# Three of seven transposes moved from TensorE to VectorE, a fourth replaced by small products, and the work of the start and the loop put in a new order

## The chip, the cores and the metric

The kernel runs on one core of one Trainium2 chip. Times are device microseconds (us). The engines are called as in the profile: PE is TensorE (the matmuls), DVE is VectorE, ACT is ScalarE, POOL is GpSimd, and SP is the engine whose queue issues nearly all DMAs here. In the traces here each engine works through its own instructions in the order in which they were written and stops at the first one that has to wait; below, four pieces of work on POOL stand 37 us behind one that waits.

A kernel's time is the median of its runs. A run counts as slow when it is over 1.5% above the fastest of its kernel. The granted clock of PE is the share of its full clock that it was given, as the profile shows it. Each profile is of one execution, whose span is 1.7 to 2.2 us shorter than the time of that run; positions in time are in a profile, counted from the start of its span. There is one profile of each kernel.

## The reference

```python
def _attn_ref(r, k, v, w, a, b):            # each (4, 8, 768, 40), float32
    state = np.zeros((B, H, D, D), dtype=np.float32)
    for t in range(S):
        kt, vt, rt = (k[:, :, t], v[:, :, t], r[:, :, t])
        wt, at, bt = (w[:, :, t], a[:, :, t], b[:, :, t])
        y[:, :, t] = np.einsum('bhd,bhde->bhe', rt, state)
        Sa = np.einsum('bhde,bhe->bhd', state, at)
        state_decay = state * wt[:, :, None, :] - np.einsum('bhd,bhe->bhde', Sa, bt)
        state = state_decay + np.einsum('bhd,bhe->bhde', vt, kt)

def _moe_ref(x, w_in, w_out):               # x (3072, 320), w_in (320, 2048), w_out (2048, 320)
    h = x @ w_in
    g = 0.5 * h * (1.0 + erf(h * inv_sqrt2))
    return (g @ w_out).astype(np.float32)
```

The recurrence's y, turned to 3072 tokens by 320, is the x of the two matrix products. `w_in` and `w_out` arrive as 64-bit floats, so the kernel makes float32 of them on the chip first.

## The kernel before

The 768 steps are cut into 12 chunks of 64. Within a chunk the recurrence is a set of small matrix products and one triangular inverse. Names that the text uses:

- *N*: a masked product of chunk c. It goes out to memory, comes back as *Nb* in another layout, and POOL (DVE for chunk 0) forms the inverse column by column. The inverse goes out and comes back as *Tt*; *L*, *J* and *J2* put its blocks together.
- *X*, *sap*, *saT*, *M*, *QY*: the chain of products of a chunk, which needs the state of the one before. X(2) is the first work of the main loop, and its start marks the end of "the start" in this document.
- *ph* and *po*: the groups of the two large products of the previous chunk, four of each per iteration, which the program puts between the small ones (`fill()`).
- *RV*, *A*, *av*, *tn*, *cum*, *ks*, *nb*: further small products, transposes and scaled operands of a chunk, called here as in the kernel; *kT*, *aT* and the like are the turned (transposed) forms of k, a and so on.
- *pieces*: `w_in` is converted in ten pieces (1 to 5 its left half, 6 to 10 its right half), `w_out` in sixteen.

A piece begins on DVE and ACT and ends either on DVE or on POOL:

```python
    def to_float(dst, words, eng):
        ...
        power = work.tile([P, LW // 2], UINT32, tag="power", name="power", bufs=2)[:, :n]
        mant = work.tile([P, LW // 2], UINT32, tag="mant", name="mant", bufs=2)[:, :n]
        nc.vector.tensor_scalar(power, hi, 0x7FF00000, None, ALU.bitwise_and)
        nc.scalar.activation(power, power, ACT.Relu, bias=rebias, scale=8.0)
        nc.vector.tensor_scalar(mant, hi, 0x000FFFFF, 0x00100000, ALU.bitwise_and, ALU.bitwise_or)
        yield
        nc.vector.scalar_tensor_tensor(power, hi, 0x80000000, power, ALU.bitwise_and, ALU.bitwise_or)
        ...
        if eng is nc.vector:
            eng.scalar_tensor_tensor(mant_f, lo, 2.0 ** -32, mant, ALU.mult, ALU.add)
            eng.scalar_tensor_tensor(dst, mant_f, 2.0 ** -20, power_f, ALU.mult, ALU.mult)
        else:
            nc.scalar.mul(lo_f, lo, 2.0 ** -52)
            nc.scalar.mul(mant_f, mant, 2.0 ** -20)
            eng.tensor_tensor(mant_f, mant_f, lo_f, ALU.add)
            eng.tensor_tensor(dst, mant_f, power_f, ALU.mult)
```

`convert(n)` runs the first half of the next piece and the second half of the piece begun before; `convert(n, True)` also ends what is begun. All turned operands come from PE, eight transposes of 128x128 each, and a copy or product out of PSUM:

```python
    def flip(src, name):
        pt = duo(name).rearrange("p g (n t) -> p g n t", n=NP)
        for g in range(G):
            for n in range(NP):
                nc.tensor.transpose(pt[:, g, n], src(g, n), ident)
        return pt
```

The start around chunk 2, and the loop's edges:

```python
    convert(1)                     # a piece of w_in; others precede
    fill()                         # ph group 1 of chunk 0
    make_M(1)
    make_y2(1)
    convert(1, True)               # ends the last piece of w_in
    turns_a(2)
    fill()                         # ph group 2
    make_N(2)
    run(start_inverse(2, nc.gpsimd))
    ...
    for c in range(2, NCH):
        ...
        if more:
            make_N(n)              # n = c + 1
            run(start_inverse(n, nc.gpsimd))
        make_X(c)
        ...
        if more2:
            turns_b(n + 1)         # kT, vT, rT
        if more:
            turn_state()
        fill()                     # the last po group
        if more:
            joined(n)              # J2
```

## Time and profile before

| | before |
|---|---|
| time, median of 3 runs before the prediction | 832.77 us |
| profiled span, mean granted PE clock | 825.5 us, 0.934 |
| X(2) starts (end of the start) | 209.5 us |
| from there to the end (the loop) | 616.0 us |
| PE busy from 200 to 820 us | 597 of 620 us |

The table is read in two parts, as the two stages have different limits. In the loop PE is the bound, so the loop shortens by what PE no longer has to do or to wait for. In the start PE is idle for more than a third of the time (busy for 131 of 209.5 us), and what counts is the chain of waits across engines and queues that ends at X(2). The prediction below shows the lines.

### The profile page before, as it was taken

What the parts mean: (1) busy time and instruction counts of PE and PEld (TensorE: products, weight loads), DVE (VectorE), ACT (ScalarE), POOL (GpSimd) and SP (SyncE); (2) the same over time, 40 slices, a digit from 0 to 9 for tenths busy, and PEclk for the clock granted to TensorE, in tenths of its full rate; (3) what the DMA queues carried; (4) which work ended last, traced back from release to release, by engine and by line L of the source; (5) the groups of instructions that cost most, each with busy time, mean ns of one, the idle gap of its engine ahead of it and who ended that gap; (6) DMA issues with size and microseconds to landing.
All of it is one profiled execution on the core that took longest, in us unless ns stands there. A gap on an engine that the chain in (4) does not pass through costs nothing.

```text
span 825.5 us, 29243 instructions
## 1 busy us (share of the span) xinstructions
PE 720.1 (87%) x13262; PEld 588.3 (71%) x13262; DVE 292.3 (35%) x452; ACT 226.8 (27%) x265; POOL 317.8 (38%) x785
## 2 busy tenths in 40 slices
PE   7427588377999999998998999999999999989997
PEld 4326467255887877877876877868878878868785
DVE  3667535856332233233233233243233333211100
ACT  4102363232232233232232232222322232102010
POOL 3380044830282281570660570660751832800000
PEclk9656779778999999999999999999999999999999
DMA  9744555733632722722712722722625322020000
GB/s 134 163 84 101 140 111 114 133 96 70 104 56 41 115 49 46 130 43 41 124 30 47 123 40 39 124 46 55 100 54 87 65 48 49 12 54 3 25 10 16
DMA packets 247820, 60.36 MB, mean 73 GB/s; under 512 B 236368, under 2 KB 240976, under 8 KB 247696
## 3 DMA queue, kind: packets, MB, share of 16 engines
q1 hardware_dynamic: 247532, 58.33, 39.4%
q8 instruction: 104, 1.70, 0.9%
q14 instruction: 20, 0.16, 0.1%
q10 hardware_dynamic: 164, 0.16, 0.1%
HBM read 44.30 MB, written 10.22 MB: 66 GB/s over the span
## 4 chain that ended last, share of the span: by engine, by line
PE 56%; POOL 12%; SPq 10%; DMA 10%; DVE 5%; issue 5%; ACT 2%; POOLq 0%; DVEq 0%; ACTq 0%
PE ph L671 20%; PE po L679 16%; POOL W L492 5%; POOL tmp L490 4%; PE QY L96 3%; SPq L639 2%; SPq L142 2%; DMA inv<-W 2%; PE J L96 2%; DMA Nb<-N 2%; DMA gt<-in_moe_w_in_dram 1%; DMA N<-N 1%; POOL st L492 1%; PE N_ps L96 1%; POOL st L490 1%
## 5 line engine op out<-in xcount | busy, mean ns | idle before, releaser
L679 PE MATMUL po<-w_out_sb,gt 128*128 128x320 f32 x768 | 223.0, 445 | 6.8 <-DVE w_out_sb L245 5.6
L671 PE MATMUL ph<-xt,w_in_sb 64*128 64x256 f32 x1920 | 223.4, 386 | 0.8 <-issue 0.8
L490 POOL TENSOR_TENSOR tmp<-W,Nb 128x126 f32<-128x126 f32 (+22 forms) x310 | 113.3, 365 | 266.7 <-DMA Nb<-N 243.1
L671 PEld LDWEIGHTS ph<-xt,w_in_sb 64*128 64x128 f32 x1920 | 185.5, 190 | 24.6 <-issue 2.4
L679 PEld LDWEIGHTS po<-w_out_sb,gt 128*128 128x128 f32 x768 | 146.9, 196 | 69.2 <-DVE w_out_sb L245 8.6
L492 POOL TENSOR_TENSOR W<-W,tmp 128x126 f32<-128x126 f32 (+22 forms) x310 | 124.4, 401 | 24.3
L673 ACT ACTIVATE gt<-ph 128x1024 f32<-128x1024 f32 x48 | 49.1, 1024 | 231.4 <-PE ph L671 231.4
L683 DVE COPY os<-po 128x320 f32<-128x320 f32 x24 | 11.8, 492 | 132.2 <-PE po L679 124.7
L629 DVE TENSOR_TENSOR y<-QY,y 128x512 f32<-128x512 f32 x22 | 15.1, 687 | 77.1 <-PE QY L96 77.1
L414 DVE TENSOR_TENSOR A<-A_ps,upper 128x1024 f32<-128x1024 f32 x12 | 14.7, 1224 | 61.5 <-PE A_ps L96 61.5
L371 POOL TENSOR_TENSOR ks<-k_raw,part 128x640 f32<-128x640 f32 x11 | 21.2, 1928 | 31.7 <-ACT part L343 25.2
L414 DVE TENSOR_TENSOR SM<-M_ps,upper 128x1024 f32<-128x1024 f32 x12 | 14.7, 1224 | 52.5 <-PE M_ps L96 52.5
L96 PE MATMUL J<-L,N 32*32 32x32 f32 x768 | 9.6, 201 | 27.1 <-DVE L L529 27.1
L96 PEld LDWEIGHTS J<-L,N 32*32 32x32 f32 x768 | 8.6, 113 | 32.1 <-issue 32.1
L414 DVE TENSOR_TENSOR VR<-RV_ps,upper 128x1024 f32<-128x1024 f32 x12 | 14.7, 1224 | 47.2 <-PE RV_ps L96 47.2
L464 ACT COPY avs<-av 128x640 f32<-128x640 f32 x12 | 8.3, 692 | 80.5 <-PE av L96 80.5
L96 PE MATMUL av<-VR,A 64*64 64x40 f32 x768 | 15.3, 240 | 15.8 <-POOL st L492 14.4
L96 PEld LDWEIGHTS av<-VR,A 64*64 64x64 f32 x768 | 13.9, 149 | 20.1 <-POOL st L492 14.6
L238 ACT ACTIVATE power<-power,rebias 128x320 uint32<-128x320 uint32 (+1 forms) x26 | 16.1, 624 | 42.7 <-DVE power L237 42.7
L96 PE MATMUL RV_ps<-rT,vT 40*64 40x64 f32 x768 | 15.6, 237 | 11.1 <-ACT rT L405 11.1
L96 PEld LDWEIGHTS RV_ps<-rT,vT 40*64 40x64 f32 x768 | 13.8, 149 | 14.9 <-ACT rT L405 11.9
L382 DVE TENSOR_TENSOR aT<-aT_ps,wpT 128x1024 f32<-128x1024 f32 x12 | 14.7, 1224 | 26.8 <-ACT wpT L380 23.6
(138 smaller groups left out, 950.7 us busy)
## 6 DMA issues: line engine op xcount, KB each, us to landing
Nb<-N SPq DMA_DIRECT2D x22, 256.0 KB
v_pad<-in_v_dram SPq DMA_DIRECT2D x48, 80.0 KB
r_pad<-in_r_dram SPq DMA_DIRECT2D x48, 80.0 KB
out_dram<-os SPq DMA_DIRECT2D x48, 80.0 KB
w_raw<-in_w_dram SPq DMA_DIRECT2D x22, 160.0 KB
b_raw<-in_b_dram SPq DMA_DIRECT2D x22, 160.0 KB
a_pad<-in_a_dram SPq DMA_DIRECT2D x22, 160.0 KB
k_raw<-in_k_dram SPq DMA_DIRECT2D x22, 160.0 KB
```

Source lines behind the costliest of these rows:

```text
L96: nc.tensor.matmul(o, lhsT, rhs, start=first, stop=True, skip_group_check=True)
L142: eng.dma_start(out=t[half(e)].rearrange("p g h d -> p (g h) d")[:, g::2, :D], in_=rows[:, H * g:H * (g + 1)])
L238: nc.scalar.activation(power, power, ACT.Relu, bias=rebias, scale=8.0)
L371: nc.gpsimd.tensor_tensor(ks[:, :, :, :D], raws.pop((c, "k")), rwv, ALU.mult)
L414: nc.vector.tensor_tensor(to, pt, upper.unsqueeze(1).to_broadcast([P, 2 * G * NP, C]), ALU.mult)
L490: eng.tensor_tensor(t, W[:, :rows, j:j + 1].to_broadcast([P, rows, rest]), Nb[:, j:j + 1, j + 1:].to_broadcast([P, rows, rest]), ALU.mult)
L492: eng.tensor_tensor(W[:, :rows, j + 1:], W[:, :rows, j + 1:], t, ALU.add)
L629: nc.vector.tensor_tensor(y2, Y, y2, ALU.add)
L639: eng.dma_start(out=xt[own + n * i:own + n * (i + 1), NP], in_=xt[other + REST:other + D, i])
L671: nc.tensor.matmul(ph[:, x, s], w_in_sb[half(x), kt, p * P:(p + 1) * P], xt[half(x), kt], start=kt == 0, stop=kt == NK - 1)
L673: nc.scalar.activation(gt[:, 4 * q:4 * q + 4].rearrange("p (x s) t -> p x s t", x=2), ph, ACT.Gelu)
L679: nc.tensor.matmul(po[:, g], gt[:, f, g * P:(g + 1) * P], w_out_sb[:, f], start=f == 0, stop=f == NF - 1)
```

## The change

The intent is to take PE work out of the loop. a, v and r are loaded in another layout ("pairs") that lets DVE's 32x32 block transpose give the turned operand, straight into SBUF. The running sums of log w are no longer transposed: PE sums them in turned form, by 64 small products. The state's part of y (y2) is summed by PE into the PSUM banks of QY, so that its own copy and additions fall away. VR gets its own load of v. N of the next chunk moves to an earlier place in the loop. And the start is written anew: pieces that ended on DVE now end on POOL, and loads and stores have other places in SP's queue.

```diff
@@ the turning of operands
-        (nc.scalar.copy if c < 3 else nc.vector.tensor_copy)(vT, flip(by_place(v_), "vT_ps"))
+    def turn(to, c, n):
+        nc.vector.transpose(to.rearrange("p n (s y) -> p n y s", y=2),
+                            raws.pop((c, n)).rearrange("p n (y d) -> p n y d", y=2)[:, :, :, :BL])
...
+        pt = duo("wT_ps").rearrange("p e (n t) -> p e n t", t=C)
+        for n in range(G * NP):
+            for x in range(2):
+                for e in range(2):
+                    at = (2 * n + x) * D
+                    mm(pt[half(x), e, n], logw[half(e), at:at + HP], cum_m[half(e), half(e)])
...
@@ y2, in the banks of QY (make_QY then adds to them: first=False)
-        pt = duo("y2_ps").rearrange("p g (i e t) -> p g i e t", i=NP, e=2)
-        for g, i, x, e, q, m in units():
-            mm(pt[half(x), g, i, e], tn[half(g, D), e, i, half(x)], t["rT"][half(g, D), q, m, half(e)])
-        y2 = t["y2"] = side("y2", "late", 1)
-        nc.scalar.copy(y2, pt.rearrange("p g i e t -> p g i (e t)"))
+                        mm(t["QY"][g][half(x), e, i, D:], tn[half(g, D), e, i, half(x)],
+                           t["rT"][half(g, D), i // NA, 2 * (i % NA) + x, e], i == 0)
...
@@ the start, around chunk 2
-    first_pieces((4,), 1, nc.vector)
-    first_pieces((0, 1, 2, 3), 1, nc.gpsimd)
+    first_pieces(range(NK), 1, nc.gpsimd)
...
+    fill()
+    make_N(2)
+    run(start_inverse(2, nc.gpsimd))
     convert(1)
     fill()
-    make_M(1)
     make_y2(1)
-    convert(1, True)
-    turns_a(2)
-    fill()
-    make_N(2)
-    run(start_inverse(2, nc.gpsimd))
+    make_M(1)
+    convert(1)
...
+    turn_k(2)
+    convert(1, True)
...
@@ the loop
-        if more:
-            make_N(n)
-            run(start_inverse(n, nc.gpsimd))
         make_X(c)
...
         if more2:
-            turns_b(n + 1)
-        if more:
-            turn_state()
+            turn_k(n + 1)
+            make_N(n + 1)
+            run(start_inverse(n + 1, nc.gpsimd))
         fill()
```

## The prediction

> **What bounds the kernel now.** I first read the forty slices, for the stages.
>
> ```profile
> PE   7427588377999999998998999999999999989997
> POOL 3380044830282281570660570660751832800000
> PEclk9656779778999999999999999999999999999999
> ```
>
> A slice is 20.6 us. TensorE (PE) is over 90% busy at full clock from slice 11 on, and sparse at a reduced clock before that. So there are two stages with different limits. The sums over stretches (length, then busy us of PE, PEld, DVE, ACT, POOL, then clock, DMA share, GB/s) put sizes on them:
>
> ```profile
> 140.00:200.00 60.00, 34.62 (x352) 23.80 (x350) 43.70 (x86) 17.23 (x25) 28.89 (x65) 0.74 0.55 119
> 200.00:820.00 620.00, 597.18 (x10996) 491.30 (x10997) 173.60 (x216) 160.73 (x179) 239.64 (x606) 0.99 0.34 59
> ```
>
> From 200 us on, PE works 597 of 620 us, and no other engine reaches 40%: a loop bound by PE, where only PE work removed is time removed. Between 140 and 200 us PE works 35 of 60 while DVE works 44: that stage waits for the conversion of the second weight matrix on DVE.
>
> Second, the PE groups, for what the loop's PE time is made of (count | busy us, mean ns | idle before):
>
> ```profile
> L96 PE MATMUL saT_ps<-Tt,part 64*64 64x64 f32 x704 | 14.3, 231 | 0.0
> L351 PE MATMUL rT_ps<-ident,r_pad 128*128 128x128 f32 x96 | 13.4, 286 | 5.9 <-DMA r_pad<-in_r_dram 5.9
> L351 PE MATMUL vT_ps<-ident,v_pad 128*128 128x128 f32 x96 | 12.6, 274 | 3.2 <-DMA v_pad<-in_v_dram 3.2
> L351 PE MATMUL aT_ps<-ident,a_pad 128*128 128x128 f32 x88 | 11.5, 274 | 2.1 <-DMA a_pad<-in_a_dram 2.0
> ```
>
> These means overlap in time; what counts is the pace from one group's start to the next. At full clock the PE timeline gives vT at 439.82, rT at 440.70, tn at 441.57: 0.87 us for eight transposes. A group of 64 small matmul records (saT, N, RV, M) takes 1.09 us in the chain. One iteration sums to about 56.7 us of such paces (ph 18.1, po 17.4, seven transposes 6.2, the rest 15), and iterations follow each other after 58 to 63 us; the difference is a wait of 1.29 us at J in nearly every one, plus instruction-issue gaps of 1 to 1.6 us in some.
>
> Third, the start, from the timelines of POOL, PE and DVE:
>
> ```profile
> 125.22 1.27 POOL L250 TENSOR_TENSOR w_in_sb<-mant,power 128x512 f32<-128x512 f32 x1
> 126.42 0.53 POOL L480 MEMSET W<- 128x512 f32 x1
> ...
> 137.76 0.24 POOL L490 TENSOR_TENSOR tmp<-W,Nb 128x31 f32<-128x31 f32 x1 [10.47 <-DMA Nb<-N]
> ...
> 168.34 0.23 POOL L492 TENSOR_TENSOR W<-W,tmp 128x16 f32<-128x16 f32 x1
> ```
>
> ```profile
> 127.09 4.59 PE L671 MATMUL ph<-xt,w_in_sb 64*128 64x256 f32 x40
> ...
> 134.62 4.59 PE L671 MATMUL ph<-xt,w_in_sb 64*128 64x256 f32 x40
> ```
>
> ```profile
> 127.21 1.23 DVE L414 TENSOR_TENSOR N<-N_ps,upper 128x1024 f32<-128x1024 f32 x1 [1.37 <-PE N_ps L96]
> ```
>
> Before, POOL finishes the last piece of the first weight matrix at 126.5 us and only then begins the inverse of chunk 2; PE's third and fourth ph groups (127.09, 134.62) come right behind the pieces. The inverse starts 9.3 us after the end of the N mask (128.44 to 137.76) and takes 30.7 us while DVE is busy.
>
> **What the Trainium skill says.** "VectorE: DVE Perf Modes", The three transpose paths: VectorE transposes only 32x32 blocks, and lands in SBUF, where TensorE's transpose lands in PSUM and needs a copy. The trace has such a transpose, L: 128x512 in 0.702 us. The product-wise DVE instructions take 0.82 us for 640 columns and 1.22 for 1024, so I estimate 1.24 us for 128x1024. "SBUF — State Buffer", two separate sides: a DVE instruction with two SBUF inputs and a GpSimd instruction that reads SBUF lock each other out. The trace agrees: in the first inverse on DVE 126 columns cost 0.29 us before POOL's inverse runs beside it and 0.36 to 0.37 after. "TensorE: Matmul & The Clock Gate", why this matters: idle gaps over about 3 us bring the array back to half clock. The trace agrees: after the 8.76 us gap before RV at 152.5 us, the 1.16 us group takes 1.99.
>
> **The change, part by part.**
>
> *PE in the loop.* The transposes of a, v and r leave PE: 3 x 0.87 = 2.6 us per chunk. The turned sums are no longer 8 transposes (0.88) but 32 products of 64x64, that is 64 records like saT, 1.09: +0.2. y2 keeps its 64 records and only changes its target. Net -2.4 us for each of the 8 iterations that still prepare a later chunk: -19. One N group of 1.09 moves out of the loop into the start: -1. The last iteration's wait at J (3.36 us) should become the usual 1.3, because its N and inverse now start almost an iteration earlier: -2. Against that, two more v loads per chunk stand in the SP queue ahead of the inverse's store, about 1.5 us of issue, of which 0.8 is won back because the outputs no longer need an addition first: J waits perhaps 0.3 longer, +2 in all. Loop: -20 us.
>
> *DVE, ACT, POOL in the loop.* DVE gains a transpose and an SBUF multiply of the old length (vT and rT copies were 1.22 each already), and loses the sums' copy (0.82) and two additions (2 x 0.69). ACT loses the 1.01 us y copy, POOL two copies of 0.45. All of it lies beside PE, which is the bound: worth nothing by itself. The PSUM pair that y2 now holds earlier leaves two of four buffers for M and ph, whose readers need 1.2 us each beside products of 2.2 us or more: no wait expected.
>
> *The start.* Here the listing of the new order decides. POOL's order becomes: pieces 1 to 5 of the first weights (left half), ks of chunk 2, piece 6, then the whole inverse of chunk 2, then pieces 7 to 10. PE's third ph group needs pieces 6 to 10. So PE must wait there for N(2), its trip through memory, the inverse and four pieces. My chain, with the durations of before:
> - The first N mask ends about 16 us (17.5 before), as a and b load ahead of k; the inverse on DVE, 22.6 us, ends near 50; the first state is out near 79.5 (80.8 before).
> - DVE then does outputs 2.2, turns of v and r 2.5, L 0.7: 85. Behind it J, tn, RV, av, X, cum, turned sums, sap, saT follow on PE to about 95, then nb, the turn of a and its scaling (3.3 us), and piece 5 waits for them on DVE and ACT and ends on POOL near 105. First ph done 109 (115 before), N(2) masked 111.5 (128.4 before).
> - Inverse: + 9.3 trip + 27.5 (27.4 in chunk 1 with DVE partly busy) = 148. Four pieces of 2 x 1.28 us are 10.2, but there are two buffers of power and mant, so pieces 9 and 10 start their DVE and ACT parts only when 7 and 8 are finished: about 13. End 161.5. Rest of ph, fourth ph, QY(1): 3 + 4.5 + 3 = 172. PE has stood still about 40 us; before, it had QY(1) and the fourth ph behind it at 139.
> - From there DVE has 15 pieces of the second weights at 2.05 us (the time with POOL idle, as at 171 to 196 us; 2.75 beside an inverse) = 31, outputs 3.6, turns 2.5, masks 2.4, nb, turn and scaling of a 3.3: 43, plus some 5 of waits for raw weights (6 before). Then 9 to 10 us of J, kT, N, po, J2. X(2), the loop's first work, starts at 172 + 57 = 229 us; before it started at 209.5. Start: +19.5 us.
>
> Sum: +19.5 - 20 = about 0, on 832.8. I put it at 831.
>
> **Rivals.** *The start costs nothing*: if the new order reaches X(2) at about 210, the loop's -20 shows bare, 812 us. For it: N(2) is 16 us earlier and the conversion no longer runs beside an inverse. Against it: POOL is in order, and pieces 7 to 10 stand behind the inverse. *The DMA queue becomes the loop's bound*: a loop's loads take 16 issues before and 28 after (issues of 0.4 to 1 us, and an SP already busy some 30 of 58 us); if J waited 3 us longer per iteration, 9 x 3 = +27, about 858. Against it: the inverse now starts some 8 us earlier, and 0.8 is won at the outputs. *The start is worse than summed*: the pieces of the second weights begin late and a cold PE takes twice as long for ph; X(2) at 245 gives 848.
>
> **Range and chances.** The start's two long terms (N(2) at 111.5, then the DVE tail) are each good to some 7 us, so the start to 10; the loop to 5. Range 808 to 848. Faster by over 2% means below 816: it needs X(2) before about 214. I give that 0.23, slower by over 2% (above 849) 0.10.
>
> **What would show it.** Right: POOL's four piece instructions after the inverse of chunk 2, PE idle some 40 us in the third ph with POOL as the releaser, X(2) near 229, iterations of 57 us instead of 59, wT_ps groups at 1.09 us pace, no aT, vT, rT on PE. Wrong: the third ph close behind the second, X(2) before 214, DVE transposes far from 1.24 us, or waits at J above 3 us.

## The result, and the profile after

The changed kernel takes 841.17 us (median of 4 runs, 839.78 to 842.48); the kernel before, in the same rounds, 832.31 us (4 runs). The ratio is 1.0113 with a 95% interval of 1.0066 to 1.0161. A ratio is the mean time of one kernel's fast runs over that of the other's of the same rounds, so it isn't quite the ratio of the medians.

| profile | before | after | difference | predicted |
|---|---|---|---|---|
| X(2) starts | 209.5 | 254.3 | +44.8 | +19.5 |
| from there to the end | 616.0 | 583.8 | -32.2 | -20 |
| span | 825.5 | 838.1 | +12.6 | about 0 |

Both halves have the predicted sign, and both are larger than predicted. The profiled run of before took 827.27 us, 5.5 less than the median of its runs, and that of after 839.78, 1.4 less than its median; so some 4 of the 12.6 us of the span come from which execution was profiled.

The forty slices of the changed kernel (21 us each; busy tenths of PE and POOL, granted clock of PE):

```profile
PE   7236771165669999999999999999999999999997
...
POOL 4282336620105507418246074182461751810000
PEclk8555595575859999999999999999999999999999
```

From slice 13 on the loop is full, and no 8 stands in it any longer, as three did before. Slices 7 and 8 are new: PE is busy for a tenth of them while POOL is busy for six tenths, with its inverse. The sums over the same stretches as before:

```profile
140.00:200.00 60.00, 20.13 (x336) 15.86 (x336) 20.73 (x39) 11.20 (x17) 24.39 (x47) 0.61 0.16 40
200.00:820.00 620.00, 593.26 (x11444) 475.52 (x11445) 194.78 (x259) 161.06 (x187) 230.12 (x594) 0.97 0.41 78
```

Between 140 and 200 us PE did 34.6 us of work before and does 20.1 now; DVE's 43.7 have become 20.7. The work wasn't saved, it was pushed back.

**The loop.** The groups that took the place of PE's transposes (count | busy us, mean ns of one | idle before):

```profile
L424 DVE TENSOR_TENSOR aT<-aT,wpT 128x1024 f32<-128x1024 f32 x12 | 24.0, 2001 | 1.6 <-ACT wpT L380 0.4
...
L166 DVE STREAM_TRANSPOSE vT<-v_pairs 128x1024 f32<-128x1024 f32 x12 | 14.5, 1212 | 0.2 <-issue 0.2
...
L100 PE MATMUL wT_ps<-cum_m,w_tile 64*64 64x64 f32 x704 | 14.0, 230 | 0.0
```

The aT_ps, vT_ps and rT_ps groups of PE are gone. A DVE transpose of 128x1024 takes 1.21 us. In the PE timeline of an iteration, the turned sums start at 345.52 and the next group at 346.61: 1.09 us, as a group of 64 small products should. X starts at 254.34, 310.40, 366.47 and so on, exactly 56.06 us apart; before, the distances were 58.1 to 63. Part of that unevenness were gaps like this one, in the PE timeline of before (the bracket has the idle time in front of the instruction; "issue" means that it waited for nothing that the profile shows):

```profile
387.73 0.83 PE L96 MATMUL X<-st,aT 40*64 40x40 f32 x42 [1.32 <-issue]
```

Before has seven such gaps after 209 us, 6.9 us in all (1.18, 1.32, 0.78, 1.59, 0.28, 0.70, 1.08). The changed kernel has none there.

**The start.** The POOL timeline of the changed kernel (start, us):

```profile
117.97 1.26 POOL L282 TENSOR_TENSOR w_in_sb<-mant,power 128x512 f32<-128x512 f32 x1
119.17 0.53 POOL L536 MEMSET W<- 128x512 f32 x1
...
130.27 0.24 POOL L546 TENSOR_TENSOR tmp<-W,Nb 128x31 f32<-128x31 f32 x1 [10.22 <-DMA Nb<-N]
...
157.05 0.23 POOL L548 TENSOR_TENSOR W<-W,tmp 128x16 f32<-128x16 f32 x1
157.23 1.27 POOL L281 TENSOR_TENSOR mant<-mant,gt 128x512 f32<-128x512 f32 x1
...
171.15 1.26 POOL L282 TENSOR_TENSOR w_in_sb<-mant,power 128x512 f32<-128x512 f32 x1
```

Piece 6 ends at 119.2. Then POOL is kept for chunk 2's inverse: 10.2 us of waiting for N to come back, 27.0 us of work to 157.3. Only then do the last four pieces end, 157.23 to 172.4. The PE timeline shows what this costs:

```profile
114.30 4.72 PE L726 MATMUL ph<-xt,w_in_sb 64*128 64x256 f32 x24 [4.07 <-POOL w_in_sb L282]
...
159.61 2.08 PE L726 MATMUL ph<-xt,w_in_sb 64*128 64x256 f32 x8 [29.80 <-ACT gt L728]
164.89 1.23 PE L726 MATMUL ph<-xt,w_in_sb 64*128 64x256 f32 x4 [3.20 <-POOL w_in_sb L282]
...
172.47 8.90 PE L726 MATMUL ph<-xt,w_in_sb 64*128 64x256 f32 x64 [1.36 <-POOL w_in_sb L282]
```

PE stands 29.80, 3.20, 3.77 and 1.36 us in the third ph group, 38.1 in all. The profile names ACT for the long one. One step further back, in the waits of all engines, ACT's GELU was held by POOL in its turn, and DVE by POOL too:

```profile
DVE power L269 <- POOL w_in_sb L282: 47.7, 5, 31.9
...
ACT gt L728 <- POOL mant L281: 35.0, 1, 35.0
```

The GELU (on ACT) of the second ph group writes into `gt`, and the raw words of piece 7 lie there until POOL has read them, at 158.5; the GELU starts at 158.54. So the inverse held PE up in two ways: the third ph group needs the pieces, and the buffers of PSUM come free only when the GELU has run. No run here takes the two apart; e1 and e15 below remove both.

The stretch from the end of QY(1) to X(2) is the third thing to see. In the DVE timeline:

```profile
210.00 0.33 DVE L269 TENSOR_SCALAR power<-w_out_sb 128x320 uint32<-128x320 uint32 x1 [1.00 <-DMA w_out_sb<-in_moe_w_out_dram]
218.48 0.33 DVE L269 TENSOR_SCALAR power<-spare_raw 128x320 uint32<-128x320 uint32 x1 [6.59 <-DMA spare_raw<-in_moe_w_out_dram]
```

and in the sums over its two parts:

```profile
184.30:238.60 54.30, 29.23 (x324) 19.50 (x320) 38.08 (x86) 15.07 (x22) 2.90 (x4) 0.71 0.57 123
238.60:254.34 15.74, 14.38 (x220) 10.20 (x220) 5.10 (x7) 1.38 (x2) 0.00 (x0) 0.60 0.19 36
```

DVE works 38.1 of the 54.3 us in which it converts `w_out`; 10.7 of the rest are waits for raw words (1.00, 6.59, 0.69 and 2.39). The closing 15.7 us are PE work at a granted clock of 0.60.

### The profile page after: what moved, and what is told of

Same layout as the page of the kernel before. It is cut to its first block, busy times and chain, and to the rows that moved or that the text cites. A ratio compares the mean times of both kernels' runs of the same rounds, so it can differ in the third digit from the quotient of the medians.

```text
span 838.1 us, 30219 instructions
## 1 busy us (share of the span) xinstructions
PE 702.7 (84%) x13646; PEld 563.3 (67%) x13646; DVE 279.1 (33%) x422; ACT 214.0 (26%) x260; POOL 315.2 (38%) x781
## 4 chain that ended last, share of the span: by engine, by line
PE 73%; POOL 6%; DMA 6%; issue 5%; SPq 4%; DVE 4%; ACT 0%; POOLq 0%; DVEq 0%
PE ph L726 25%; PE po L734 24%; PE QY L100 5%; PE J L100 2%; PE N_ps L100 2%; DMA w_out_sb<-in_moe_w_in_dram 2%; PE cum L100 2%; PE M_ps L100 1%; POOL W L548 1%; POOL mant L281 1%; PE sap L100 1%; POOL tmp L546 1%; PE saT_ps L100 1%; PE X L100 1%; PE wT_ps L100 1%
## 5 line engine op out<-in xcount | busy, mean ns | idle before, releaser
L726 PE MATMUL ph<-xt,w_in_sb 64*128 64x256 f32 x1920 | 225.8, 388 | 42.2 <-ACT gt L728 29.8
L734 PE MATMUL po<-w_out_sb,gt 128*128 128x320 f32 x768 | 225.7, 448 | 9.1 <-DVE w_out_sb L277 8.0
L548 POOL TENSOR_TENSOR W<-W,tmp 128x126 f32<-128x126 f32 (+22 forms) x310 | 113.9, 368 | 24.3
L686 DVE TENSOR_TENSOR xt<-QY,wpT 128x512 f32<-128x512 f32 x24 | 15.5, 686 | 65.5 <-PE QY L100 65.5
L464 DVE TENSOR_TENSOR N<-N_ps,upper 128x1024 f32<-128x1024 f32 x12 | 14.7, 1225 | 36.0 <-PE N_ps L100 36.0
L424 DVE TENSOR_TENSOR aT<-aT,wpT 128x1024 f32<-128x1024 f32 x12 | 24.0, 2001 | 1.6 <-ACT wpT L380 0.4
```

Of the source, the lines that this page charges most:

```text
L424: nc.vector.tensor_tensor(flat_a, flat_a, wp, ALU.mult)
L464: nc.vector.tensor_tensor(to, pt, upper.unsqueeze(1).to_broadcast([P, 2 * G * NP, C]), ALU.mult)
L548: eng.tensor_tensor(W[:, :rows, j + 1:], W[:, :rows, j + 1:], t, ALU.add)
L686: nc.vector.tensor_tensor(xt[:, :NP, g * P:(g + 1) * P].rearrange("p i (e t) -> p i e t", e=2), Y, wp[:, g, :, :, :C], ALU.mult)
L726: nc.tensor.matmul(ph[:, x, s], w_in_sb[half(x), kt, p * P:(p + 1) * P], xt[half(x), kt], start=kt == 0, stop=kt == NK - 1)
L734: nc.tensor.matmul(po[:, g], gt[:, f, g * P:(g + 1) * P], w_out_sb[:, f], start=f == 0, stop=f == NF - 1)
```

## The experiments

Eleven kernels ran, in four sets; each set had its own runs of the kernel before (medians 831.49, 833.88, 833.98 and 835.89 us). The sets ran on three chips, so between sets it is the ratios that compare. All gave correct results. One more idea, a third buffer each for `power` and `mant`, did not build: the pool would need 69.8 KB per partition, and 66.9 were left.

The measured places, all from the profiles:

| kernel | median us | ratio to before (95%) | X(2) at | X(2) to end |
|---|---|---|---|---|
| before | 832.31 | 1 | 209.5 | 616.0 |
| after | 841.17 | 1.0113 (1.0066 to 1.0161) | 254.3 | 583.8 |
| e1, pieces before inverse | 808.01 | 0.9709 (0.9642 to 0.9776) | 221.2 | 583.7 |
| e2, old start | 808.43 | 0.9702 (0.9638 to 0.9766) | 223.3 | 583.7 |
| e4, y2 apart | 844.46 | 1.0130 (1.0051 to 1.0208) | 256.8 | 589.4 |
| e6, idle transposes | 863.91 | 1.0361 (1.0289 to 1.0433) | 257.1 | 605.6 |
| e7, before, loads split | 829.38 | 0.9946 (0.9895 to 0.9997) | 215.5 | 610.4 |
| e9, e1 and store first | 809.37 | 0.9703 (0.9643 to 0.9763) | 223.4 | 585.3 |
| e10, e9 and five pieces on POOL | 813.26 | 0.9745 (0.9694 to 0.9795) | 229.0 | 583.7 |
| e15, after, four pieces on DVE | 802.93 | 0.9646 (0.9594 to 0.9699) | 215.0 | 585.5 |
| e16, e15 and early store | 803.29 | 0.9648 (0.9597 to 0.9699) | 216.7 | 583.7 |
| e17, e16, all pieces on DVE | 801.68 | 0.9616 (0.9543 to 0.9689) | 219.0 | 583.7 |
| e18, before, N's place of after | 824.89 | 0.9895 (0.9845 to 0.9946) | 211.9 | 608.0 |

My theory after the result: the start lost 39 us or so to one thing, the four pieces behind the inverse in POOL's order; the loop gained from the transposes and, beyond that, from N's new place. The rivals: the start is bound by something else that the reordering shifted (raw weights, SP's queue, DVE), or the new parts themselves cost the time.

### e1: the same kernel, pieces 7 to 10 ahead of the inverse on POOL

```diff
     make_N(2)
-    run(start_inverse(2, nc.gpsimd))
+    inverse_2 = start_inverse(2, nc.gpsimd)
     convert(1)
...
     convert(1, True)
+    run(inverse_2)
     second_load(4, 6)
```

> The changed kernel with one thing moved: on POOL the last four pieces of the first weight matrix come before the inverse of chunk 2, not after it. My theory (the start's loss is that PE's third ph group waits for POOL): PE stands still at the third ph no more, QY(1) ends near 140 us instead of 184, the loop starts near 210 us instead of 254, and the time falls from 841 to about 797 (790 to 806), PE's longest wait at ph below 6 us. Rival (the conversion of the second weights on DVE bounds the start anyway): the 30 us saved at ph come back as waits at po for w_out_sb, and the time stays above 825.

Measured: 808.01 us. The long wait in the PE timeline is gone, and in the POOL timeline the inverse begins where the pieces end:

```profile
136.45 1.23 PE L726 MATMUL ph<-xt,w_in_sb 64*128 64x256 f32 x4 [3.77 <-POOL w_in_sb L282]
139.03 9.28 PE L726 MATMUL ph<-xt,w_in_sb 64*128 64x256 f32 x64 [1.36 <-POOL w_in_sb L282]
```

```profile
137.71 1.26 POOL L282 TENSOR_TENSOR w_in_sb<-mant,power 128x512 f32<-128x512 f32 x1
138.93 0.32 POOL L546 TENSOR_TENSOR tmp<-W,Nb 128x31 f32<-128x31 f32 x1
```

PE now waits 9.2 us in the third ph group instead of 38.1. QY(1) ends at 151.3 instead of 184.3 and X(2) starts at 221.2 instead of 254.3: 33 us at both places. So the order of two items in POOL's queue alone was worth 4% of the kernel. I had expected 797; the time fell 2 us outside my range, as the stretch from QY(1) to X(2) kept its 70 us.

### e15: the order untouched, pieces 7 to 10 ended on DVE

e1 changes when the inverse runs as well as when the pieces do. e15 leaves the changed kernel's order alone and takes only the pieces off POOL.

```diff
-    first_pieces(range(NK), 1, nc.gpsimd)
+    first_pieces((0,), 1, nc.gpsimd)
+    first_pieces(range(1, NK), 1, nc.vector)
```

> The changed kernel with its order untouched; only pieces 7 to 10 of the first weights end on VectorE, three instructions of 0.69 us there in place of two on VectorE's and GpSimd's sides, so that nothing of the third ph group stands behind the inverse of chunk 2 on GpSimd any longer. My theory (the 30 us of PE's stand come from GpSimd's order alone): pieces 7 to 10 are done by about 140 us beside the inverse, QY(1) ends near 150 instead of 184, X(2) near 219 instead of 254: 805 us (798 to 812). Rival: the stretch is bound by something else that the pieces-first experiment moved along with it (the arrival of the raw weights, or VectorE itself, now with two SBUF inputs beside GpSimd's inverse): over 820 us.

Measured: 802.93 us, the middle of the range. In its PE and POOL timelines:

```profile
130.18 0.70 PE L726 MATMUL ph<-xt,w_in_sb 64*128 64x256 f32 x4 [1.38 <-DVE w_in_sb L277]
133.10 1.23 PE L726 MATMUL ph<-xt,w_in_sb 64*128 64x256 f32 x4 [2.22 <-DVE w_in_sb L277]
135.21 9.06 PE L726 MATMUL ph<-xt,w_in_sb 64*128 64x256 f32 x64 [0.88 <-DVE w_in_sb L277]
...
214.96 1.14 PE L100 MATMUL X<-st,aT 40*64 40x40 f32 x64
```

```profile
130.13 0.24 POOL L546 TENSOR_TENSOR tmp<-W,Nb 128x31 f32<-128x31 f32 x1 [10.44 <-DMA Nb<-N]
...
160.99 0.23 POOL L548 TENSOR_TENSOR W<-W,tmp 128x16 f32<-128x16 f32 x1
```

The inverse starts where it did (130.1) and takes longer, 31.1 us instead of 27.0, with DVE now at work beside it, but PE no longer waits behind it here. The last piece ends at 135.2 on DVE instead of 172.4 on POOL, and X(2) comes at 215.0. One edit takes 39.4 us out of the start. This settles the cause: POOL's order, not the arrival of the weights and not DVE, which took on these pieces with 4.5 us of waits of PE for them left in the group. It is also a kernel that beats both: 3.5% faster than before.

### e2: all the new parts with the start order of before

The start of before was put back, with the new parts in it (DVE transposes, turned sums, y2 in QY's banks, the loads in pairs); the loop is that of after. The edit is the whole start, so its rule stands here for it: each call of before, in the order of before, with DVE's turns of v and r of chunk 0 behind the first inverse.

> All parts of the change (turns on DVE, products for the turned sums, y2 in the shared banks) and its loop, but the order of the start as in the kernel before. My theory (the parts are good, the start's order is what loses): the loop starts near 208 us and lasts 584 as in the changed kernel, time about 797 (788 to 806), 4% faster than before. Rival (the parts themselves slow the start: v loaded twice, three more turns on a DVE that is busy there): the loop starts after 235 us and the time is above 820.

Measured: 808.43 us, outside my range. X(2) comes at 223.3, which is 13.8 us later than in before. So the new parts (with one N group moved into the start, 1.1 us) cost the start some 14 us even in the old order, and my 797 had overlooked it. N of chunk 0 is masked 4.1 us later (at 20.38 instead of 16.30); then in the SP timeline the loads of VR and v hold the queue for 6.4 us (23.60 to 29.96) where before had 2.6; behind them stands the return of N, and the first inverse starts at 34.7 instead of 28.3. The loads of chunk 1 hold it for 10.5 us again (64.87 to 75.32, before 6.3), and L of chunk 1 is 17.7 us late (108.49 instead of 90.83). How much each new part costs was not tested. The new order of after avoids the late first inverse (it ends at 49.2, here at 57.2). Whether the new order as a whole is better is less clear: e1, with the inverse behind the pieces, reaches X(2) only 2.1 us before e2, and e15, 8 us before it, also ends other pieces on DVE than e2 does.

### e6: three groups of idle transposes put back into the loop

```diff
             turn_k(n + 1)
+            for _ in range(3):
+                flip(by_pair(turned_in[n + 1]["ks"]), "idle_ps")
             make_N(n + 1)
```

> The changed kernel with three idle groups of eight PE transposes put into each of the eight loop iterations that prepare a later chunk, read by nobody: only the PE work that the change took out comes back. My theory (the loop is bound by PE, each group is worth its pace of 0.87 us): +2.6 us for each of 8 iterations, 841 + 21 = 862 (858 to 866), iterations of 58.7 us instead of 56.1. Rival (PE has slack in the loop, which takes part of it): below 852.

Measured: 863.91 us, with iterations of 58.7 to 58.9 us instead of 56.06. The PE timeline has the added group:

```profile
306.74 2.78 PE L388 MATMUL idle_ps<-ident,ks 128*128 128x128 f32 x24
```

Three groups of eight transposes cost 2.7 us an iteration (the loop is 21.8 us longer than that of after, over 8 iterations), as the pace of 0.87 us says. A transpose taken from PE is worth its whole pace in this loop.

### e4: y2 in its own bank again

```diff
+        pt = duo("y2_ps").rearrange("p g (i e t) -> p g i e t", i=NP, e=2)
+        for g, i, x, e, q, m in units():
+            mm(pt[half(x), g, i, e], tn[half(g, D), e, i, half(x)], t["rT"][half(g, D), q, m, e])
+        y2 = t["y2"] = side("y2", "late", 1)
+        nc.scalar.copy(y2, pt.rearrange("p g i e t -> p g i (e t)"))
...
+            if state[0] is not None:
+                y2 = t["y2"][:, g].rearrange("p i (e t) -> p i e t", e=2)
+                nc.vector.tensor_tensor(y2, Y, y2, ALU.add)
+                Y = y2
```

The order of M and y2 is that of before too.

> The changed kernel with y2 summed apart again (own bank, ACT copy of 1.0 us, two DVE additions of 0.7 us per chunk). My theory (ACT and DVE work beside a loop bound by PE is worth nothing): 841 to 846, at most 0.5 us per chunk for the later xt. Rival (the shared banks save what the ACT and DVE work costs, 2.4 us per chunk): 11 x 2.4 = 26 us more, 867.

Measured: 844.46 us. The iterations are 56.20 to 56.23 us long, 0.15 more than in after. One alone took 59.55: its last po group ran 7.06 us instead of 4.47 with no wait before it, at a granted clock of 0.64. Such a group at a lower granted clock stands once or twice in some profiles (an iteration 1.6 us longer in e9 and e15, a group 1.7 us longer in before), whatever the kernel; why was not tested. In the last iteration that waits at J the wait is 2.09 us instead of 1.29. The copy on ACT and the additions on DVE that the change saves lie beside PE, which has as many products either way. The summing in QY's banks is worth little by itself, about 2 us in all.

### e7 and e18: why PE's issue gaps left the loop

The transposes explain 8 times 2.35 to 2.4 us of the loop's 32. What of the rest? e7 took the kernel before and cut its loads of w, a, b and k from 160 KB to 80 KB.

```diff
         for e in range(2):
-            eng.dma_start(out=t[half(e)].rearrange("p g h d -> p (g h) d")[:, :, :D], in_=rows_of(src, c, e))
+            for g in range(G):
+                eng.dma_start(out=t[half(e)][:, g, :, :D], in_=rows_of(src, c, e)[:, H * g:H * (g + 1)])
```

> The kernel before, its start order and its loop, with one edit: each large load of w, a, b and k (160 KB) is cut in two, so that no load is larger than 80 KB, as in the changed kernel. My theory: the gaps of 0.3 to 1.6 us in PE's instruction issue in the loop of before (6.9 us in its trace, none in the changed kernel's) come from instruction fetches that queue behind large loads; they then go, and the time falls by 4 to 9 us (ratio 0.989 to 0.995). Rival: the gaps depend on the number of PE instructions or on their place in the loop and not on the loads; then they stay, and the time is the same within 3 us (ratio 0.997 to 1.003), or worse by the extra issues.

Measured: a ratio of 0.9946 (0.9895 to 0.9997). The number alone lies in my theory's range and not in the rival's; but the gaps are still there, three of four in the same place, X:

```profile
218.00 0.44 PE L96 MATMUL X<-st,aT 40*64 40x40 f32 x5 [1.46 <-issue]
```

Four gaps of 4.0 us (1.46, 0.25, 1.06, 1.21) are left of seven of 6.9. The expectation also held a mistake: the changed kernel still has loads of 160 KB (w, b, k, VR), so load size could not have been the difference between the two kernels. The theory falls; why e7's loop is 5.6 us shorter than that of before, with 2.9 us less of gaps, was not followed up. A look at the DMA load of before from 386 to 389 us, in slices of 75 ns, says the same of the gap that ended at 387.73: from 386.5 to 387.2 no DMA engine is busy.

```profile
DMA  4898720000000000595992100000000015887787
```

e18 tests the next idea: in before, J2, N and X follow each other, 192 small products in a row; in after N has moved ahead of the last po group, and only 128 follow each other. e18 is the kernel before with that move alone.

```diff
         more, more2 = n < NCH, n + 1 < NCH
-        if more:
-            make_N(n)
-            run(start_inverse(n, nc.gpsimd))
         make_X(c)
...
             turns_b(n + 1)
+            make_N(n + 1)
+            run(start_inverse(n + 1, nc.gpsimd))
         if more:
             turn_state()
```

> The kernel before with its transposes, its start order and its loads; only the place of N and of the start of its inverse in the loop is the changed kernel's: behind kT, vT and rT of the next chunk, ahead of the last po group, instead of between the last J products and X. My theory: the changed kernel's loop gains 19.3 us from the transposes, and the other 13 us of its 32 come from this move: the 192 small products in a row (J, N, X) in which PE's instruction issue has its gaps become 128 (no gaps any more, -6.9 us), J waits 1.3 us in every iteration, the last too (-3), and one N group leaves the loop for the start (+1 there). Time: 8 to 11 us less than before (ratio 0.986 to 0.991), gaps under 1 us in all. Rival: the gaps come with the transposes or with the loads of before; then they stay (4 to 7 us), and the time falls by 2 to 4 us at most (ratio 0.995 to 0.998).

Measured: a ratio of 0.9895, and in the loop's PE timeline a single gap is left, at another place:

```profile
636.85 0.33 PE L96 MATMUL A_ps<-aT,kT 40*64 40x64 f32 x5 [0.96 <-issue]
```

Most iterations are now 58.41 us long; 58.41 less 56.06 is 2.35, which the other parts of the change save, the transposes above all. The loop is 8.0 us shorter than that of before, from N's place alone. That N's move removes the gaps at X is shown, as far as one profile of each kernel can; why PE is left without instructions there is not. The Trainium skill, "Runtime: NRT & Kernel Launch", Instruction fetch mechanics, says that an engine's instructions come in blocks of 16 KiB, 256 instructions, over a queue of their own. Before has 104 packets and 1.70 MB on its queue of kind "instruction", and 13262 matmuls with as many weight loads are 103.6 blocks. The page calls the cost "mostly hidden". The traces hold one thing more. Each of the seven gaps of before, of the four of e7 and the one of e18 ends 2.3 to 3.0 us after the start of a packet of 16 KB on that queue, and 1.2 to 1.6 us after its end; in before such packets are some 7 us apart in the loop. For the gap that ends at 387.73 the packet runs from 385.29 to 386.17, in the DMA load from 385 to 386:

```profile
q8 instruction: 1, 0.02, 5.5%
```

With their weight loads, 192 small products are 384 instructions, more than a block; 128 are 256, one block. So a block that comes late in a long row of small products is the likely cause of the gaps. That is read from when the packets come; no run changed the fetching alone, so it is not shown.

### e9, e16, e17: three further edits to the start that bring little

e9 is e1 with the eight loads of the last fifth of `w_in` moved behind the store and fetch of the first inverse. SP had stood in them for 11.6 us (43.85 to 55.45), while the inverse was ready at 49.2.

```diff
-    first_load(True, 0, early(4))
     run(inverse)
     store_inverse(0)
...
     fetch_inverse(0)
+    first_load(True, 0, early(4))
```

> The pieces-first order, and besides the eight loads of the last fifth of the first weights are moved in SP's queue from before the store of the first inverse to after its fetch. My theory: in the changed kernel the store was issued 6 us after the inverse ended because SP stood in these loads; so everything behind it (first state, first ph group) comes some 5 us earlier, and X(2) at about 216 instead of 221: 803 us (799 to 807). Rival: the start is bound from elsewhere (the conversion chain on DVE, ACT and POOL, and the arrival of raw weights), then the gain is lost before X(2): 807 to 809.

Measured: 809.37, no gain. In its SP timeline the store is 4.9 us earlier:

```profile
50.69 1.28 SPq L560 DMA_DIRECT2D inv<-W  x2
```

But L, which needs the fetched inverse, comes at 62.45 instead of 62.90. On DVE the mask of A for chunk 1 stands ahead of it, waiting for PE until 61.31. A later wait took the place of the removed one, as the rival said.

e16 is e15 with chunk 1's inverse stored ahead of v(1) and the next raw weights:

```diff
     fetch_inverse(0)
+    store_inverse(1)
     load_v(1)
```

> As the kernel with pieces 7 to 10 on VectorE, and besides the store of chunk 1's inverse stands in SP's queue ahead of the loads of v(1) and of the next first weights. In the changed kernel GpSimd stood 12.4 us before its memset, from the end of that inverse (66) to the landing of its store (78), and VectorE 5.5 us behind it. My theory: the memset runs at about 72, the first pieces come 5 us earlier, and the first ph group 2 to 4 us earlier: 802 us, 2 to 4 us below the other. Rival: the first pieces after these two are held by their places in VectorE's order (7.2, 5.8 and 5.4 us of waits of GpSimd for ACT's part of a piece), and v(1) and the raw weights now come later: the same within 2 us, or slower.

Measured: 803.29, the same. The POOL timeline shows both halves of the rival:

```profile
69.60 0.42 POOL L835 MEMSET st<- 128x384 f32 x1 [3.77 <-DMA inv<-st]
...
94.31 1.28 POOL L281 TENSOR_TENSOR mant<-mant,w_out_sb 128x512 f32<-128x512 f32 x1 [12.01 <-ACT mant L280]
```

The memset is 8.8 us earlier than in e15 (78.35), and the first piece 4.1, but the third piece starts at 94.31 (93.55 in e15): it waits for its place on DVE, whose order has the products of chunk 1 in between.

e17 is e16 with all ten pieces of `w_in` ended on DVE (`nc.gpsimd` becomes `nc.vector` in both calls of `first_pieces`).

> As the kernel with the early store, and all ten pieces of the first weights end on VectorE. My theory: the fifth piece ends 2 us earlier (its way to GpSimd falls away) and no piece waits for the memset, but the start gets about 1.4 us of work more on VectorE per piece: about the same, 800 us (796 to 806). Rival: VectorE is what the stretch from 70 to 120 us waits for, then 5 pieces of 1.4 us are added there: 807 to 812 us.

Measured: 801.68; its interval overlaps those of e15 and e16. POOL's part in these pieces no longer matters.

### e10: five pieces of the second weights ended on POOL

```diff
-    second_pieces((*range(NF - 2), NF - 1, NF - 2), nc.vector)
+    second_pieces(range(6), nc.vector)
+    for f in (*range(6, NF - 2), NF - 1, NF - 2):
+        second_pieces((f,), nc.gpsimd if f % 2 else nc.vector)
```

> As the store-first kernel, and five of the sixteen pieces of the second weights end on GpSimd, which is idle there, instead of on VectorE (two instructions of about 0.49 us less on VectorE per piece). My theory: the stretch of 70 us from the end of QY(1) to X(2) is bound by VectorE, which goes from piece to piece; it shortens by about 4 us, to about 799 us (795 to 803). Rival: the stretch waits for the raw weights on the DMA queues, or the two SBUF inputs of GpSimd's and VectorE's instructions lock each other out and give it back: no gain, or a loss, 802 to 810.

Measured: 813.26, against 809.37 for e9, on which it builds. PE takes the pieces in order, and those from POOL are the ones that it waits longest for:

```profile
209.46 1.44 PE L734 MATMUL po<-w_out_sb,gt 128*128 128x320 f32 x2 [4.52 <-POOL w_out_sb L282]
```

The waits for POOL are 2.76, 2.82 and 4.52 us; those for DVE in the same stretch of e9 are 1.12 to 2.79. Less work on DVE did not help. I think that each piece takes longer on its way and that only two can be under way (two buffers); a lock between DVE and POOL, my rival, was not ruled out. Either way the 70 us are not bound by DVE's busy time alone. What would shorten them is left open: in after, e1, e2, e9, e15 and e17 alike the stretch from QY(1) to X(2) is 67.7 to 70 us long.

## Why the prediction was right or wrong

The predicted 831 us against 841 measured: within the range, and within 2%, as thought most likely. But that the sum came so near was luck: two errors of opposite sign met, as the start was 25.3 us worse than predicted and the loop 12.2 us better. Point by point:

**Right in mechanism and size**
- *The transposes* (-2.6 us per chunk, the turned sums +0.2): 2.35 us an iteration between e18 and after, 2.7 in e6.
- *DVE's transpose of 128x1024* (1.24): 1.20 to 1.25.
- *DVE, ACT and POOL beside PE are worth nothing*: e4 shows it for y2, 0.15 us an iteration.
- *N out of the loop* (-1), *the last J wait* (-2): 3.36 has become 1.29. The size is right, the reason only in part: with N early and nothing else (e18) the wait is still 2.64, and with all but the summing of y2 in QY's banks (e4) it is 2.09, 0.80 more than in after, as much as the prediction had put down to the outputs.
- *POOL's order*: the inverse between pieces 6 and 7, PE standing about 40 us in the third ph group. It stood 38.1. The inverse's trip (9.3) took 8.9 us from the end of N's mask (121.4) to 130.27, the inverse (27.5) 27.0. The first mask (16) ended at 16.07, the first inverse (near 50) at 49.2. That this part made the changed kernel slower is shown by e1 and e15.

**Terms of the start that were too small**
- *From L of chunk 1 to saT in 10 us (85 to 95).* L ended at 87.7, saT's products at 107.3: 19.6 us. PE had just waited 6.6 us for L and went on at half its pace: tn 1.97 us, RV 1.99, X 1.92, cum 2.50, where the loop has 1.09, 1.16, 1.14 and 1.34. In the PE timeline, and in the sums from 88 to 107 us:

```profile
87.86 1.08 PE L100 MATMUL J<-L,N 32*32 32x32 f32 x64 [6.63 <-DVE L L585]
88.87 1.97 PE L388 MATMUL tn_ps<-ident,st 128*128 128x128 f32 x8
...
96.95 1.92 PE L100 MATMUL X<-st,aT 40*64 40x40 f32 x64
...
106.43 0.85 PE L100 MATMUL saT_ps<-Tt,part 64*64 64x64 f32 x37 [1.14 <-issue]
```

```profile
88.00:107.00 19.00, 16.56 (x521) 14.27 (x518) 7.00 (x12) 9.04 (x13) 6.60 (x5) 0.57 0.66 138
```

PE was busy for 16.6 of these 19 us and its granted clock was still 0.57. The prediction quoted the clock gate from the skill and did not use it on its own chain. Gaps of 1.30 and 1.14 us come on top. So piece 5 ended at 114.2 instead of 105, and N(2) was masked at 121.4 instead of 111.5. This is 9.9 of the 25.3 us; 2.7 of it is L itself, which ended at 87.7 instead of 85.
- *Four pieces done from 148 to 161.5, 10.5 us more to QY(1)'s end*: 15.2 and 11.9. With 0.9 us given back by the inverse and its trip, this is about 2.4 more: QY(1) ended at 184.3 instead of 172.
- *The DVE tail of 57 us*: 70. The busy part was even smaller (38.1, not 43), but the waits were 16.2 (54.3 less 38.1) instead of 5, above all for raw weights (10.7), and the closing part on PE took 15.7 instead of 9 to 10, at a clock of 0.60. This is the other 13 us. What bounds these 70 us stays open.

**Terms of the loop**
- *J waits 0.3 us longer, +2 in all*: wrong. J waits 1.29 us in every iteration; before, some waits were 1.8 and the last 3.36. Two more loads in SP's queue cost nothing there. The rival of the DMA queue as the loop's bound did not come about.
- *Issue gaps*: the prediction named them as part of an iteration and gave the change no credit for removing them. They were 6.9 us in the profile of before, and e18 shows that N's new place ends most of them (0.96 us is left).
- The sum of the loop: 8 times 2.4 for the transposes is 19.3, N 1.1, gaps 6.9, J waits 3.1, and one ph group of before at a lower clock (at 388.49, 6.27 us instead of 4.59) 1.7: 32.1 of the measured 32.2. The fit is better than the parts deserve: a po group of before at 734.35 ran 1.4 us long as well and is not in the sum.

*The scaling of a, "of the old length",* was wrong without consequence. It takes 2.39 us in each of the eight iterations, beside POOL's scaling of k, and 1.23 alone in the start:

```profile
291.64 0.82 DVE L407 SCALAR_TENSOR_TENSOR nb<-b_raw,part 128x640 f32<-128x640 f32 x1 [2.52 <-ACT part L378]
291.68 2.18 POOL L413 TENSOR_TENSOR ks<-k_raw,part 128x640 f32<-128x640 f32 x1 [7.33 <-ACT part L378]
292.56 2.39 DVE L424 TENSOR_TENSOR aT<-aT,wpT 128x1024 f32<-128x1024 f32 x1
```

All three read two SBUF operands: it is the lock that the prediction cites from "SBUF — State Buffer", and the times fit a full block by whichever starts first, to within 0.15 us. nb has its 0.82 us; ks takes 0.65 more than its 1.53 alone, where 0.78 of nb were left when it started; aT takes 1.16 more than its 1.23, where 1.30 of ks were left.

Two readings of the prediction are off without consequence: three of the slices from 11 on show 8 and not 9, and the issue gaps run from 0.28 to 1.59 us, not from 1 to 1.6.

In short: the step that decided the sign, POOL's order, was read right before the run. What failed were sums of durations taken from a busy PE and a well-fed DVE, for a stage in which PE runs at half pace and raw words come late.

## What to carry to other kernels

Before giving an engine more work, list what already stands in its queue and what each item waits for: an item that depends on a round trip through memory blocks everything written behind it, and here four pieces of 2.6 us each stood 37 us behind one. Moving them to an engine whose order did not hold them up (one edit) turned a loss of 1.1% into a gain of 3.5%. And sum a sparse stage with durations from a sparse stage: here half-pace matmuls and waits for loads made most of the 23 us that were added to a chain that had been built from the numbers of a busy one.

## What the Trainium skill lacked or had wrong

- "VectorE: DVE Perf Modes", The three transpose paths: its table gives bf16 at 128x128 only. In float32 eight PE transposes of 128x128 have a pace of 0.87 us in the loop, and one DVE transpose of 128x1024 takes 1.20 to 1.25 us, about as long as a product of that length (1.22).
- "Runtime: NRT & Kernel Launch", Instruction fetch mechanics: no warning that a long row of small matmuls can leave PE without instructions. Seven gaps of 0.28 to 1.59 us in one loop, one of 0.96 us after N was moved, each ending 2.3 to 3.0 us after a block's packet began.
- "TensorE: Matmul & The Clock Gate", why this matters: it names gaps of over about 3 us. It holds here (X at 1.92 us after a gap of 6.6 us, 1.14 in the loop), but a sparse stage whose clock goes up and down (0.58 from 195 to 209 us, 1.00 from 209 to 218, 0.60 from 238.6 to 254.3) deserves a line on how to estimate it.
- "DMA: Bandwidth & Descriptors" has no figure for loads whose issue holds the issuing engine up: eight issues that follow eight loads under way took 11.6 us on SP instead of about 4 (4.0 in e9).
